# Summing phi(k) over the tokens with a matrix of ones: two fp32 products become four float32r products

## The chip, the cores and the metric

The kernel runs on one core of a Trainium2 chip. The metric is the device time of one execution in microseconds (us), as the median of several runs. The engines are PE (TensorE, the matrix engine), DVE (VectorE), ACT (ScalarE), POOL (GpSimd) and SP (SyncE, which here only issues DMAs); PEld stands for the weight loads of PE. "fp32r" in rows of the profile and "f32r" or "float32r" in the text mean the reduced-precision float32 type of matrix products.

## The reference

Two kinds of block alternate on one sequence of 2048 tokens with 640 channels: A, B, A, B, with the same weights both times, and each block normalizes its input and adds its result to that input.

```python
phi = lambda t: jnp.where(t > 0, t + 1, jnp.exp(t)) + 1e-6
pq, pk = phi(q), phi(k)                       # 32 heads of 20 channels
kv = jnp.einsum("bhsd,bhse->bhde", pk, v)
z = jnp.einsum("bhsd->bhd", pk)               # sum of phi(k) over all tokens
num = jnp.einsum("bhqd,bhde->bhqe", pq, kv)
den = jnp.einsum("bhqd,bhd->bhq", pq, z)[..., None] + 1e-6
o = num / den                                 # then o @ wo
...
r = max(x @ w1 + b1, 0);  out = (r * r) @ w2 + b2     # block B, 1728 hidden
x = x + A(layernorm(x)); x = x + B(layernorm(x))      # twice
```

The change concerns z alone.

## The kernel before

The tokens are 16 tiles of 128 (`NT`), the 640 channels five chunks of 128 (`DC`) or two halves of 320 (`HD`). The kernel goes through two layers; a layer is one block A and one block B. The order of the instructions on each engine is the order of the code: the work is interleaved by hand.

Matrix products are made in float32r from two parts. `split` (L125 to L128) writes a high part, an ACT copy rounded to float32r, and a low part, a DVE subtract of the high part from the source. `mm3` (L379) then makes three products: high by low, low by high, high by high.

Block A goes over the tiles. For each it projects k, and q for most tiles; ACT takes the exponential (L475) and DVE the rest of phi (L482, L483). In `k_post` phi(k) of the tile is split into `kh` (ACT L646, DVE L653), and between the two POOL adds it to the running sum `acc` (L648 for the first tile, L650 for the others): acc[p, c] is the sum over the 16 tiles of phi(k) at row p. With the split normalized input `xh`, PE gathers G and GT, from which k'v is made. The pool function `xtile` hands out eight buffers in rotation to xh and kh, and afterwards to the tiles kvbd, Mr and pT.

For six tiles of each layer q is left out of this loop (`LATE`). These late parts come behind it, two per tile, through `late_q`: 15 products into one of three PSUM banks that `xbank` hands out in rotation, the exponential, the rest of phi, and after the second half a store by SP.

Behind the first two late parts comes the place of the change: a product of a 128x128 matrix of ones with `acc` sums over the 128 rows and puts the sum into every row, so that `zbc` holds z for all partitions.

```python
late_q(2)
zbc = tmp.tile([P, D], F32, tag="z", name="zbc", bufs=1)
psz = [xbank()[:, :HD] for _ in range(2)]
for j in range(2):
    nc.tensor.matmul(psz[j], ones, acc[:, j * HD : (j + 1) * HD], start=True, stop=True)   # L804
for j in range(2):
    nc.scalar.activation(zbc[:, j * HD : (j + 1) * HD], psz[j], AF.Copy)                   # L806
b_den(0)
```

`b_den` (DVE, L582 `pr` and L585 `den`) uses zbc for the denominators. On PE the last G part (`g_part(15)`), the last GT part (added into GT on DVE, L513), another late part, the products for kv (L852) and M (L865) follow, with ACT copies (G of L810, Mc of L871) and small DMAs that shift M into its tiles (Mr); then the first output tiles, whose residual is added on DVE (L621), and ACT's block moves (z of L365), and then block B: fc1 (L1005), fc2 (L1055).

The matrix `ones` is filled by POOL (L539) at the start of each layer. In layer 0 that code stands behind the start-up: the wqkv chunks are loaded (`st`) and split (`kq`, L128), tiles 0 and 1 are normalized (DVE L336, L338, L346 with POOL L340, L341), and tile 1 is transposed on PE (L350) and split into xT.

Of the kernel before, what the change touches and what calls it, by code (L numbers as in the profile page):

```python
# [8 lines left out]
F32 = mybir.dt.float32  # L9
R32 = mybir.dt.float32r  # L10
# [3 lines left out]
P = 128  # L14
# [4 lines left out]
HD = D // 2  # L19
# [52 lines left out]
def kernel(  # L72
# [11 lines left out]
    nc = tc.nc  # L84
# [3 lines left out]
    cpool = ctx.enter_context(tc.tile_pool(name="cpool", bufs=1))  # L88
# [18 lines left out]
    make_identity(nc, ident)  # L107
    neghalf = cpool.tile([P, 1], F32, name="neghalf")
    nc.vector.memset(neghalf, -0.5)
    b2bc = cpool.tile([P, D], F32, name="b2bc")  # L110
    b1sb = cpool.tile([P, NF], F32, name="b1sb")

# [8 lines left out]
    def ftile(name):  # L121
        return tmp.tile([P, D], F32, tag="f", name=name, bufs=F_BUFS)


    def split(hi, lo, src):  # L125

        nc.scalar.activation(hi, src, AF.Copy)
        nc.vector.tensor_tensor(out=lo, in0=src, in1=hi.bitcast(F32), op=ALU.subtract)  # L128
# [283 lines left out]
    def a_load(t, src):  # L412
        if t < NT:
            xt[t] = ftile("xt")
            nc.sync.dma_start(xt[t], src[t])
# [16 lines left out]
    for layer in range(N_LAYERS):  # L432
# [6 lines left out]
        ap = sg.enter_context(  # L439
            tc.tile_pool(name=f"a_{layer}", bufs=1, side="left", reuse_waits="tile")  # L440
        )
# [7 lines left out]
        acc = ap.tile([P, D], F32, name="acc", tag="acc", bufs=1)  # L449
# [4 lines left out]
        def xbank():  # L454
            xbanks.append(xbanks.pop(0))
            return bank(xbanks[-1])

        def part(t, a, b, ps=None):

            ps = (xbank() if ps is None else ps)[:, : b - a]  # L460
            for c in range(DC):
                mm3(
                    ps, xT[t][:, 0, c, :], xT[t][:, 1, c, :],
                    kq[c][:, 0, a:b], kq[c][:, 1, a:b], c == 0, c == DC - 1,
                )
            return ps
# [23 lines left out]
        def xtile(name, dtype=R32):  # L490
            return xp.tile([P, 2, D], dtype, tag="x", name=name, bufs=8)
# [23 lines left out]
        if layer == 0:  # L515
# [19 lines left out]
            a_apply(1)  # L535
            first_loads.step(3, 5)
            a_load(2, src)
        ones = ap.tile([P, P], F32, name="ones", tag="ones", bufs=1)
        nc.gpsimd.memset(ones, 1.0)  # L539
        mask = ap.tile([HR, 6, DH], F32, name="mask", tag="mask", bufs=1)  # L540
        nc.gpsimd.memset(mask, 1.0)

# [235 lines left out]
        def late_q(n=1, rest=True):  # L778

            for _ in range(n):  # L780
                if not late_parts:
                    return
                t, j = late_parts.pop(0)
                if j == 0:
                    late_phi[t] = Phi(ftile("rl"))
                late_phi[t].exp(j * HD, part(t, D + j * HD, D + (j + 1) * HD))
                late_todo.append((t, j))
                if rest:
                    late_rest()
# [3 lines left out]
        def late_rest(n=9):  # L793
            for _ in range(min(n, len(late_todo))):
                t, j = late_todo.pop(0)
                late_phi[t].rest()
                if j == 1:
                    nc.sync.dma_start(pqd[t], late_phi.pop(t).r)

        late_q(2)  # L800
        zbc = tmp.tile([P, D], F32, tag="z", name="zbc", bufs=1)
        psz = [xbank()[:, :HD] for _ in range(2)]
        for j in range(2):
            nc.tensor.matmul(psz[j], ones, acc[:, j * HD : (j + 1) * HD], start=True, stop=True)  # L804
        for j in range(2):
            nc.scalar.activation(zbc[:, j * HD : (j + 1) * HD], psz[j], AF.Copy)  # L806
        b_den(0)
# [729 lines left out]
```

## Time and profile before

| | before |
|---|---|
| time, median of 3 runs | 1353.05 us (1352.7 to 1353.13) |
| time of the profiled execution | 1352.46 us |
| its span, first to last instruction | 1350.5 us |
| granted PE clock | 1.0 |
| PE busy | 1342.5 us |
| DVE busy | 912.1 us |
| ACT busy | 770.2 us |
| POOL busy | 122.6 us |
| the two fp32 products, per layer | 4 records, from 193.10 and from 860.25 us |

Rows of the profile give a start (us from the span's start) and a duration, the engine, the line, the operation and its tiles, out<-in, with partitions x elements; x15 counts instructions. What stands in square brackets is the engine's idle time before it and what ended it. In the chain of work that ended last, each piece is what the end of the kernel was waiting for at that time.

### The profile page before, as it was taken

How to read it: one execution, taken by the hardware profiler on the slowest of the kernel's cores; microseconds unless marked ns; L12 is line 12 of the kernel's file. 1: busy time of each engine (PE TensorE's matmuls, PEld its weight loads, DVE VectorE, ACT ScalarE, POOL GpSimd, SP SyncE). 2: the span in 40 equal slices, each digit the busy share in tenths (PEclk: the TensorE clock that was granted, in tenths of full speed). 3: DMA queues.
4: the chain of work that ended last, by engine and by line, in shares of the span. 5: the costliest groups of instructions: out<-in, count | busy, mean ns of one | idle time of the engine just before them, and what ended most of it. 6: DMA issues, size and time to landing. Idle time of an engine off the chain costs nothing.

```text
span 1350.5 us, 19013 instructions
## 1 busy us (share of the span) xinstructions
PE 1342.5 (99%) x6817; PEld 1160.9 (86%) x6817; DVE 912.1 (68%) x1625; ACT 770.2 (57%) x1931; POOL 122.6 (9%) x174
## 2 busy tenths in 40 slices
PE   9999999999999999999999999999999999999998
PEld 8888998988888888888888899988888888888887
DVE  7888757777777676643467676677778667775323
ACT  5888858566546447411447688495756446464110
POOL 2222210000000000000012232100000000000000
PEclk9999999999999999999999999999999999999999
DMA  6787834574665484387521115156546646654744
GB/s 205 254 296 271 282 92 169 195 280 141 212 242 167 159 297 167 116 326 297 185 98 41 58 40 156 40 205 253 172 160 235 212 148 224 234 168 139 287 126 157
DMA packets 85635, 253.44 MB, mean 188 GB/s; under 512 B 11030, under 2 KB 19606, under 8 KB 84902
## 3 DMA queue, kind: packets, MB, share of 16 engines
q1 hardware_dynamic: 85398, 252.04, 53.8%
q8 instruction: 54, 0.88, 0.3%
q14 instruction: 39, 0.32, 0.1%
q10 hardware_dynamic: 144, 0.20, 0.0%
HBM read 193.50 MB, written 56.03 MB: 185 GB/s over the span
## 4 chain that ended last, share of the span: by engine, by line
PE 92%; DVE 4%; ACT 3%; issue 1%; POOL 0%; DMA 0%; DVEq 0%; ACTq 0%; POOLq 0%
PE PS L379 34%; PE PS L1005 28%; PE PS L1055 28%; ACT z L365 2%; PE PS L852 1%; PE PS L865 1%; DVE bn L336 0%; PE PS L521 0%; DVE kq L128 0%; DVE e L482 0%; DVE xr L621 0%; DVE r L483 0%; DVE xTb L128 0%; DMA Mr<-Mc 0%; POOL rs L341 0%
## 5 line engine op out<-in xcount | busy, mean ns | idle before, releaser
L365 ACT ACTIVATE z<-y 32x160 f32<-32x160 f32 x1424 | 475.9, 334 | 75.7 <-DVE y L356 59.4
L1005 PE MATMUL PS<-xTb,u 128*128 128x512 f32 x1400 | 333.8, 390 | 1.0 <-DVE xTb L128 1.0
L1005 PEld LDWEIGHTS PS<-xTb,u 128*128 128x128 f32 x1400 | 261.7, 188 | 54.9 <-DVE xTb L128 1.5
L379 PE MATMUL PS<-kq,xT 128*128 128x320 f32 (+2 forms) x1635 | 294.0, 334 | 1.1 <-DVE kq L128 0.6
L379 PEld LDWEIGHTS PS<-kq,xT 128*128 128x128 f32 x1635 | 259.0, 188 | 28.9 <-DVE rl L483 1.0
L1055 PE MATMUL PS<-u,h 128*128 128x512 f32 x1120 | 276.8, 390 | 0.0
L1055 PEld LDWEIGHTS PS<-u,h 128*128 128x128 f32 x1120 | 208.6, 188 | 40.8
L1017 ACT ACTIVATE hr<-PS,b1sb 128x512 f32<-128x512 f32 x104 | 71.4, 686 | 295.7 <-PE PS L1005 295.0
L1018 DVE TENSOR_TENSOR hr<-hr 128x512 f32<-128x512 f32 x104 | 71.8, 691 | 218.3 <-ACT hr L1017 217.9
L379 PE MATMUL PS<-kh,xh 128*128 128x512 f32 x480 | 124.3, 393 | 0.0
L475 ACT ACTIVATE e<-PS 128x320 f32<-128x320 f32 (+4 forms) x128 | 53.6, 435 | 102.5 <-PE PS L379 99.0
L340 POOL TENSOR_SCALAR rs<-mv 128x1 f32<-128x1 f32 x64 | 28.0, 438 | 871.1 <-DVE mv L338 871.1
L379 PE MATMUL PS<-uM,pT 128*128 128x320 f32 x648 | 102.6, 309 | 0.7 <-DVE uM L881 0.7
L379 PEld LDWEIGHTS PS<-uM,pT 128*128 128x128 f32 x648 | 97.7, 188 | 3.1 <-DVE uM L881 1.2
L379 PEld LDWEIGHTS PS<-kh,xh 128*128 128x128 f32 x480 | 87.4, 188 | 15.0
L482 DVE TENSOR_SCALAR e<-e 128x320 f32<-128x320 f32 (+4 forms) x128 | 42.6, 333 | 79.6 <-ACT e L475 79.2
L1055 PE MATMUL PS<-h,u 128*128 128x512 f32 x280 | 79.0, 390 | 0.0
L1020 DVE TENSOR_TENSOR h<-hr,h 128x512 fp32r<-128x512 f32 x104 | 72.0, 692 | 3.6
L650 POOL TENSOR_TENSOR acc<-acc,r 128x640 f32<-128x640 f32 x30 | 53.8, 1792 | 199.1 <-DVE r L483 199.1
L1055 PEld LDWEIGHTS PS<-h,u 128*128 128x128 f32 x280 | 52.2, 188 | 10.8 <-DVE h L1031 0.4
L1005 PE MATMUL PS<-xTb,uw 128*128 128x512 f32 x240 | 57.1, 389 | 0.0
L483 DVE SCALAR_TENSOR_TENSOR r<-PS,e 128x512 f32<-128x512 f32 (+2 forms) x104 | 51.1, 492 | 5.8 <-ACT e L475 2.3
(119 smaller groups left out, 1337.6 us busy)
## 6 DMA issues: line engine op xcount, KB each, us to landing
u<-kept_w SPq DMA_DIRECT2D x184, 640.0 KB, 4.7
x<-x SPq DMA_DIRECT2D x48, 320.0 KB, 5.7
kept_w<-uprep SPq DMA_DIRECT2D x23, 640.0 KB, 4.7
pqt<-pq SPq DMA_DIRECT2D x32, 320.0 KB, 4.6
x<-xr SPq DMA_DIRECT2D x32, 320.0 KB, 3.9
st<-in_B_w_dram SPq DMA_DIRECT2D x22, 320.0 KB, 5.8
pq<-r SPq DMA_DIRECT2D x20, 320.0 KB
kept_kq<-kq SPq DMA_DIRECT2D x10, 640.0 KB, 6.8
```

The lines of the kernel that those rows point to most:

```text
L340: nc.gpsimd.tensor_scalar(rs, mv[:, 1:2], LN_EPS, None, op0=ALU.add)
L365: nc.scalar.activation(zv[j * B32 : (j + 1) * B32, :, i, :], yv[i * B32 : (i + 1) * B32, :, j, :], AF.Copy)
L379: nc.tensor.matmul(ps, a, b, start=first and i == 0, stop=last and i == 2)
L475: nc.scalar.activation(self.e[:, a:b], ps, AF.Exp)
L482: nc.vector.tensor_scalar(e, e, 1.0, PHI_EPS, op0=ALU.min, op1=ALU.add)
L483: nc.vector.scalar_tensor_tensor(out=self.r[:, a:b], in0=ps, scalar=0.0, in1=e, op0=ALU.max, op1=ALU.add)
L650: nc.gpsimd.tensor_tensor(out=acc, in0=acc, in1=r, op=ALU.add)
L1005: nc.tensor.matmul(ps, a[:, d, :], bb[:, d, :], start=d == 0 and i == 0, stop=d == DC - 1 and i == len(seq) - 1,)
L1017: nc.scalar.activation(r, ps, AF.Relu, bias=b1sb[:, c : c + 1])
L1018: nc.vector.tensor_tensor(out=r, in0=r, in1=r, op=ALU.mult)
L1020: nc.vector.tensor_tensor(out=h[:, 1], in0=r, in1=h[:, 0].bitcast(F32), op=ALU.subtract)
L1055: nc.tensor.matmul(ps, l, r, start=first and k == 0, stop=last and k == len(a) - 1)
```

## The change

The running sum is split in two parts, as other operands of products are: `ah` holds the float32r copy of acc (ACT) and the rest (DVE). It is made between the first and the second late part. The matrix of ones becomes float32r; it is no longer filled by POOL but copied by DVE from a new constant column of ones. Each half of z is then the sum of two products, ones by the low part and ones by the high part, into one bank.

```diff
@@ constants
     nc.vector.memset(neghalf, -0.5)
+    one = cpool.tile([P, 1], F32, name="one")
+    nc.vector.memset(one, 1.0)
@@ start of each layer
-        ones = ap.tile([P, P], F32, name="ones", tag="ones", bufs=1)
-        nc.gpsimd.memset(ones, 1.0)
+        ones = ap.tile([P, P], R32, name="ones", tag="ones", bufs=1)
+        nc.vector.tensor_copy(ones, one.to_broadcast([P, P]))
@@ behind the loop over the tiles
-        late_q(2)
+        late_q(1)
+        ah = xtile("ah")
+        split(ah[:, 0], ah[:, 1], acc)
+        late_q(1)
         zbc = tmp.tile([P, D], F32, tag="z", name="zbc", bufs=1)
         psz = [xbank()[:, :HD] for _ in range(2)]
         for j in range(2):
-            nc.tensor.matmul(psz[j], ones, acc[:, j * HD : (j + 1) * HD], start=True, stop=True)
+            for i in (1, 0):
+                nc.tensor.matmul(
+                    psz[j], ones, ah[:, i, j * HD : (j + 1) * HD], start=i == 1, stop=i == 0
+                )
```

## The prediction

> **What bounds the kernel now.** I read the page first: busy times, then the chain of work that ended last.
>
> ```profile
> PE 1342.5 (99%) x6817; PEld 1160.9 (86%) x6817; DVE 912.1 (68%) x1625; ACT 770.2 (57%) x1931; POOL 122.6 (9%) x174
> ...
> PE 92%; DVE 4%; ACT 3%; issue 1%; POOL 0%; DMA 0%; DVEq 0%; ACTq 0%; POOLq 0%
> ```
>
> TensorE (PE) holds 92% of that chain and waits almost nowhere, at a granted clock of 1.0 throughout. So time taken off PE where PE carries the chain comes off the end, and a wait put on PE there is added to it. The products that change are those of L804, once per layer. The chain of work in order of time shows them in layer 0:
>
> ```profile
> 180.81 12.46 PE PS L379 x75
> 193.26 1.08 PE PS L804 x4
> 194.34 7.41 PE PS L379 x42
> ```
>
> They lie on the chain, with PE work on both sides. Each fp32 product leaves two records, so 2 products are 4 records and cost 1.08 us. Layer 1 is the same (1.08 us at 860.41). The third view is the timeline around them:
>
> ```profile
> 185.81 0.73 ACT L127 ACTIVATE xh<-xt 128x640 fp32r<-128x640 f32 x1
> ...
> 186.31 0.49 DVE L483 SCALAR_TENSOR_TENSOR r<-PS,e 128x320 f32<-128x320 f32 x1
> 186.72 0.81 DVE L128 TENSOR_TENSOR xh<-xt,xh 128x640 fp32r<-128x640 f32 x1
> ...
> 186.95 2.01 POOL L650 TENSOR_TENSOR acc<-acc,r 128x640 f32<-128x640 f32 x1 [5.67 <-DVE r L483]
> 187.61 2.03 DVE L653 TENSOR_TENSOR kh<-r,kh 128x640 fp32r<-128x640 f32 x1
> ...
> 188.71 4.56 PE L379 MATMUL PS<-kq,xT 128*128 128x320 f32 x30
> 191.10 0.44 ACT L475 ACTIVATE e<-PS 128x320 f32<-128x320 f32 x1 [3.52 <-PE PS L379]
> ...
> 191.93 0.49 DVE L483 SCALAR_TENSOR_TENSOR rl<-PS,e 128x320 f32<-128x320 f32 x1
> 192.96 0.87 PEld L804 LDWEIGHTS PS<-acc,ones 128*128 128x128 f32 x4
> 193.10 1.24 PE L804 MATMUL PS<-acc,ones 128*128 128x320 f32 x4
> ```
>
> The reader sees here all that the change needs: the last addition to acc on POOL is over at 186.95 + 2.01 = 188.96; PE is busy with two late parts (30 products) until L804; an ACT copy and a DVE subtract of the wanted shape stand at 185.81 and 186.72; and the same subtract took 2.03 instead of 0.81 where it ran beside POOL's addition. The last view is the chain at the start of the kernel, since one added instruction lies there:
>
> ```profile
> 15.11 2.47 DVE kq L128 x3
> 17.58 0.25 DVE e L482
> ...
> 19.89 3.44 PE PS L379 x14
> ```
>
> There VectorE (DVE), not PE, carries the chain: PE waits until 19.89 for the low part of xT of tile 1, which stands in DVE's queue behind the three subtracts and the two phi halves.
>
> **The change part by part.**
>
> The products. Thirty f32r products of 320 columns take from 188.71 to 193.10, so 4.39/30 = 0.146 us each. Four are 0.585 us where two fp32 ones took 1.08: **0.50 us less per layer** if nothing waits. The records stay at four per layer. By the Trainium skill (FP8 and Floating Point Precision, TensorE Precision Notes) a true fp32 product is four passes through the array; a pass would then be 1.08/8 = 0.135, four of them 0.54, an estimate, and the saving 0.54 instead of 0.50. The row of the f32r product itself is what I use.
>
> The wait in front of them. Before, L804 waited for POOL's sum, done 4 us earlier. Now its first product needs the low part of ah, that is: exp of the first late part, ACT copy, DVE subtract, PE. ACT's exp starts at 191.10; the copy of xh began 0.33 after the exp ahead of it (185.48 to 185.81), so the copy of ah begins at 191.43 and ends 0.73 later at 192.16. On DVE the subtract stands behind the phi operation of 191.93; at 186.31 the next one began 0.41 later, so it begins at 192.34 (the copy is done by then) and ends 0.81 later at 193.15. From a DVE end to the released weight load of PE the trace shows 0.05 us (h of L1031 ends at 676.72, the load starts at 676.77). So the weight load of L804 starts at 193.20 instead of 192.96: **0.24 us of waiting per layer**. Bounds: nothing, if DVE's part slips under PE's late parts; 1.46 us, if the subtract takes 2.03 as at 187.61. I take 0.24, since POOL has nothing to do here, as at 186.72, where 0.81 was measured.
>
> Who stands behind the waits: on PE, behind L804, the 15 products of the last G part and the ACT evictions of G that they release; they move with it. On ACT the copy lies in an idle stretch of 1.76 us ahead of the second exp (193.30), which it leaves at 192.16. On DVE the subtract lies in an idle stretch of 1.35 us ahead of 193.77 and is over at 193.15, so the store of the late phi on SP and the first pr are not later. The copies of zbc (193.84, 194.3) need the first two products, ready at about 193.34 + 0.29 + 0.2 = 193.8 as before. All of that costs nothing; if the cover on ACT or DVE were gone, each step would cost its own 0.73 or 0.81 on PE.
>
> Net at this place: -0.50 + 0.24 = -0.26 per layer, **-0.51** for two. What follows is a chain of PE work (G, kv, M) released by PE itself until 219, and the DVE and ACT work after it is released by PE, so the shift should reach the end.
>
> The matrix of ones. POOL loses a fill of 0.20 us per layer; POOL is idle 91% of the span, so nothing is gained. DVE gets a copy of 128x128 with rounding. In layer 1 it stands behind the residual additions that end at 681.1, and DVE is idle until 683.89: nothing. In layer 0 it stands between the third kq subtract (ends 17.58) and the phi operation of 17.50, on the chain. The trace has no such copy. A DVE operation of 128x128 took 0.23 (L482 at 686.97), a fill of one column 0.06; neighbours overlap by 0.08 there. Between 0.06 and 0.23 I take 0.23 - 0.08 = **+0.15 us**, nearest to the row of equal size. The new one-column fill at the start runs while DVE waits until 3.93 for x: nothing.
>
> The tile ah takes the place of an old xh tile, and the later tiles of that pool (kvbd, Mr, pT) each move on by one place. Their former owners are read last by the G and GT parts that end near 200, and the new users come after 202: nothing. The new column of ones moves nearly all other SBUF tiles by 32 bytes (tmp tiles from offset 224 to 0 within 256). I cost that at nothing; it is a rival below.
>
> Sum: -0.51 + 0.15 = **-0.36 us**. The profiled execution took 1352.46 (span 1350.5 and 1.96 around it), so it would be 1352.1; it lies 0.59 under the median of 1353.05, and for the median I forecast 1353.05 - 0.36 = **1352.7**. A difference of 0.2%, 2.7 us, is about what a measurement of this kernel can tell from no change, and the sum is far inside it.
>
> **The rivals.**
>
> 1. No wait: the subtract ends before PE asks for it. Then 2 x 0.50 is gained and 0.15 paid, -0.84: **1352.2**. For it: only 0.24 us are missing. Against: the chain exp, copy, subtract is laid end to end from measured rows.
>
> 2. The gain does not arrive: the wait is 0.50, or the stretch from 237 to 242, where ACT's z moves carry the chain, takes back what PE gained. Left is the +0.15 of the start: **1353.2**. Against: that stretch is released by PE's product through the addition of L621.
>
> 3. Slower by a late subtract: if it runs at the 2.03 of 187.61, PE waits 1.46 instead of 0.24, +0.96 per layer, with the start +2.1: **1355.1**. It costs more than the products save from a duration of 0.81 + 0.26 = 1.07 on. For it: 2.03 is there, 5 us earlier, for an equal subtract. Against: that one lay beside POOL's addition, and the last addition is over 3.4 us before this one. The Trainium skill (SBUF — State Buffer, Who interferes with whom) has a rule for it: a DVE instruction with two SBUF inputs contends with a GpSimd instruction that reads SBUF. The trace agrees with it in the pair 186.95/187.61; it would decide only if POOL's addition ended 3.4 us later.
>
> 4. The moved addresses change the rate of every product. Column time from two rows: 15 products of 512 columns take 3.40 us (0.227 each) against 0.146 for 320, so 0.081/192 = 0.42 ns a column. One column time over 6817 records is 2.9 us. One less gives -3.2: **1349.8**; two more give +5.3: **1358.4**. For it: all f32r operands of this trace start at the same offset, so no row shows another. Against: on DVE and ACT, r (offset 192) and xt (224) cost the same, 0.81 and 0.73 to 0.75. The skill's DMA: Bandwidth & Descriptors (How a descriptor splits into AXI transactions) counts an extra transaction where a descriptor does not start on 256 B; that would shorten transfers now, but no run here shows it so far, and DMA holds 0% of the chain.
>
> That the change does not do what it says I exclude: every f32r product of 320 columns in the trace takes the 0.146.
>
> **How the numbers follow.** The forecast has 0.56; rival 1 0.15, a quarter microsecond away; rival 2 0.10; rival 3 0.04, as its cause is absent; rival 4 0.09 for faster and 0.06 for slower, since the trace can't exclude it and either sign is open. Forecast and rivals 1 and 2 span 1352.2 to 1353.2 and hold 0.81; with the scatter of the runs (1352.46 to 1353.13) and the unknown wait (0.24 us more per layer than I took is +0.5) the range is 1351.2 to 1354.2. Rivals 3 and 4 stay outside. Faster by over 0.2%: 0.09 (rival 4). Slower: 0.06 (rival 4). Within: 0.56 + 0.15 + 0.10 + 0.04 = 0.85.
>
> **What would show it.** In the profile after: four records on ah and ones, spaced 0.146 and not 0.27; their weight load 0.24 us later than before, counted from the first late part, with a wait on DVE's ah; that subtract at 0.81 (rival 3: 2 us); the chain's piece at these products down from 1.08 to some 0.6 plus 0.24 of DVE; PE's first product after xT of tile 1 about 0.15 later than 19.89; POOL 172 instructions, DVE 1630, ACT 1933. If 15 products of 512 columns no longer take 3.40, it is rival 4. The prediction is wrong if the time moves by more than 2 us either way.

## The result and the profile after

| | before | after |
|---|---|---|
| time, median of 6 runs each | 1352.93 us (1352.7 to 1353.22) | 1364.74 us (1364.3 to 1364.94) |
| ratio, after to before | | 1.0086 (95%: 1.0076 to 1.0096) |
| profiled execution, its span | 1352.46, 1350.5 us | 1364.3, 1362.5 us |
| granted PE clock | 1.0 | 0.999 |

The changed kernel is 11.8 us slower, and the forecast of 1352.7 us with its range of 1351.2 to 1354.2 was wrong. What the change itself does came out almost as worked out; the time went to products that the change does not touch.

The page of the kernel after, its busy times, the shares of the chain, and three rows of the costliest groups (row columns: busy us, mean ns of one | idle time ahead of it):

```profile
PE 1354.2 (99%) x6817; PEld 1160.0 (85%) x6817; DVE 913.8 (67%) x1630; ACT 771.2 (57%) x1933; POOL 122.4 (9%) x172
...
PE 91%; DVE 3%; ACT 3%; DMA 1%; issue 1%; POOL 0%; SPq 0%; DVEq 0%; ACTq 0%
...
L1013 PE MATMUL PS<-xTb,u 128*128 128x512 f32 x1400 | 334.9, 391 | 1.0 <-DVE xTb L130 1.0
...
L1063 PE MATMUL PS<-u,h 128*128 128x512 f32 x1120 | 282.6, 394 | 0.0
...
L1063 PE MATMUL PS<-h,u 128*128 128x512 f32 x280 | 80.7, 397 | 0.0
```

PE has the same 6817 records and 11.7 us more busy time (1342.5 to 1354.2); the other engines moved by under 2 us. So the time is not a new wait: it is inside PE's own work. The same rows of the page before:

```profile
L1005 PE MATMUL PS<-xTb,u 128*128 128x512 f32 x1400 | 333.8, 390 | 1.0 <-DVE xTb L128 1.0
...
L1055 PE MATMUL PS<-u,h 128*128 128x512 f32 x1120 | 276.8, 390 | 0.0
...
L1055 PE MATMUL PS<-h,u 128*128 128x512 f32 x280 | 79.0, 390 | 0.0
```

fc2 (u,h and h,u) alone has 5.8 + 1.7 = 7.5 us more, with as many products as before. The place that the change was made for looks as forecast. The chain after, in order of time, in layer 0:

```profile
181.84 12.48 PE PS L381 x75
194.32 0.80 PE PS L810 x4
195.12 7.37 PE PS L381 x42
```

The four records cost 0.80 instead of 1.08 us, and the 75 products ahead of them 12.48 instead of 12.46. The timeline after around them:

```profile
192.16 0.44 ACT L477 ACTIVATE e<-PS 128x320 f32<-128x320 f32 x1 [3.55 <-PE PS L381]
192.49 0.73 ACT L129 ACTIVATE ah<-acc 128x640 fp32r<-128x640 f32 x1
...
192.99 0.49 DVE L485 SCALAR_TENSOR_TENSOR rl<-PS,e 128x320 f32<-128x320 f32 x1
193.39 0.81 DVE L130 TENSOR_TENSOR ah<-acc,ah 128x640 fp32r<-128x640 f32 x1
194.26 0.59 PEld L810 LDWEIGHTS PS<-ah,ones 128*128 128x128 f32 x4 [0.21 <-DVE ah L130]
194.26 0.85 PE L810 MATMUL PS<-ah,ones 128*128 128x320 f32 x4
```

exp, copy, subtract and weight load follow each other as laid out: copy 0.33 after the exp, subtract at 0.81 and not 2.03, a wait of 0.21 on DVE's ah. And the chain after at the start of the kernel:

```profile
15.18 2.48 DVE kq L130 x3
17.65 0.14 DVE ones L541
17.79 0.24 DVE e L484
...
20.10 3.48 PE PS L381 x14
```

The copy of ones costs 0.14 us on DVE's chain; PE's first product of tile 1 starts at 20.10 instead of 19.89. All of this together is a fraction of a microsecond. The chain in the middle of block B of layer 0 shows the rest, 15 products a piece, first before:

```profile
333.90 3.40 PE PS L1005 x15
337.30 3.40 PE PS L1055 x15
```

and then after:

```profile
335.59 3.41 PE PS L1013 x15
339.00 3.50 PE PS L1063 x15
```

fc1 (L1013) runs as before, fc2 (L1063) takes 0.10 us more for every 15 products. Summed over the trace, from the start of one PE product to the start of the next (u are the streamed weights of block B and uw those that stay in SBUF, kq,xT the projections of block A, uM,pT its output product):

| group, moving operand first | spacings | before | after | difference |
|---|---|---|---|---|
| fc2 u,h 512 columns | 1119 | 227.5 ns | 232.6 ns | +5.80 us |
| fc2 h,u 512 | 280 | 228.3 | 234.1 | +1.62 |
| fc2 uw,h and h,uw 512 | 240 | 226.7 | 232.8 | +1.48 |
| fc1 xTb,u and xTb,uw 512 | 1640 | 227.5 | 228.4 | +1.34 |
| kq,xT 512 | 570 | 228.0 | 230.3 | +1.31 |
| kq,xT 320 | 780 | 151.6 | 152.0 | +0.29 |
| uM,pT 320 | 648 | 148.4 | 148.6 | +0.15 |

Together these are 12.0 us, as much as the span grew (the groups left out, the start and the gain at the changed place are each under 0.6 and nearly cancel); 11.6 of it is in products of 512 columns. A 512-column product takes 226.7 ns in its fast form (uw,h before), and near 233 in its slow one.

### The profile page after: what moved, and what is told of

Same layout as the page of the kernel before. It is cut to its first block, busy times and chain, and to the rows that moved or that the text cites. A ratio compares the mean times of both kernels' runs of the same rounds, so it can differ in the third digit from the quotient of the medians.

```text
span 1362.5 us, 19015 instructions
## 1 busy us (share of the span) xinstructions
PE 1354.2 (99%) x6817; PEld 1160.0 (85%) x6817; DVE 913.8 (67%) x1630; ACT 771.2 (57%) x1933; POOL 122.4 (9%) x172
## 4 chain that ended last, share of the span: by engine, by line
PE 91%; DVE 3%; ACT 3%; DMA 1%; issue 1%; POOL 0%; SPq 0%; DVEq 0%; ACTq 0%
PE PS L381 33%; PE PS L1063 28%; PE PS L1013 27%; ACT z L367 2%; PE PS L860 1%; DMA st<-in_A_wqkv_dram 1%; PE PS L873 1%; DVE bn L338 0%; DVE e L484 0%; DVE xr L623 0%; DVE r L485 0%; DVE xTb L130 0%; DMA Mr<-Mc 0%; PE PS L1077 0%; POOL rs L343 0%
## 5 line engine op out<-in xcount | busy, mean ns | idle before, releaser
L1013 PE MATMUL PS<-xTb,u 128*128 128x512 f32 x1400 | 334.9, 391 | 1.0 <-DVE xTb L130 1.0
L1013 PEld LDWEIGHTS PS<-xTb,u 128*128 128x128 f32 x1400 | 261.7, 188 | 56.3 <-DVE xTb L130 1.5
L1063 PE MATMUL PS<-u,h 128*128 128x512 f32 x1120 | 282.6, 394 | 0.0
L1063 PEld LDWEIGHTS PS<-u,h 128*128 128x128 f32 x1120 | 208.3, 187 | 47.0
L1063 PE MATMUL PS<-h,u 128*128 128x512 f32 x280 | 80.7, 397 | 0.0
L1063 PEld LDWEIGHTS PS<-h,u 128*128 128x128 f32 x280 | 52.2, 188 | 11.6 <-DVE h L1039 0.3
L1013 PE MATMUL PS<-xTb,uw 128*128 128x512 f32 x240 | 57.2, 390 | 0.0
```

The costliest lines, as they stand in the source:

```text
L1013: nc.tensor.matmul(ps, a[:, d, :], bb[:, d, :], start=d == 0 and i == 0, stop=d == DC - 1 and i == len(seq) - 1,)
L1063: nc.tensor.matmul(ps, l, r, start=first and k == 0, stop=last and k == len(a) - 1)
```

## The experiments

SBUF tiles are handed out from both ends of a partition, left-hand pools upwards and right-hand ones downwards. Theory A: the new column of ones shifts the other tiles of the left-hand side of SBUF by 32 bytes, against the tiles of block B's pool, which lie on the right-hand side (weights u on the left, h on the right), and that makes 512-column products slower. The rival, theory P: the work that the change adds or moves (split, copy of ones, the four products) does it.

**The column of ones alone** (to the kernel before):

```diff
+    one = cpool.tile([P, 1], F32, name="one")
+    nc.vector.memset(one, 1.0)
```

> The kernel before with nothing but the new constant column of ones and its fill: the products, the split and the matrix of ones stay as before, but nearly all tiles of the left-hand pools start 32 bytes later, as in the changed kernel. Theory A (addresses: the moved tiles slow the float32r products, the products of ones are nearly free): about 1365, fc2 products spaced 232 to 234 ns instead of 227. Theory P (the new products, split or copy disturb PE's rhythm, addresses don't matter): 1352.9, spacing 227.

Measured: 1365.37 us against 1352.99, ratio 1.0092 (1.0075 to 1.0108). One unused column costs all of it.

**The whole change, with addresses as before** (to the kernel after: the ones share a tile with a constant that was there):

```diff
-    neghalf = cpool.tile([P, 1], F32, name="neghalf")
+    consts = cpool.tile([P, 2], F32, name="consts")
+    neghalf = consts[:, 0:1]
...
-    one = cpool.tile([P, 1], F32, name="one")
+    one = consts[:, 1:2]
```

> The changed kernel with both one-column constants in one tile of two columns, so that every other tile keeps the address it had before. Theory A: the local sum of the prediction comes out, about 1352.6 (0.36 less than before), fc2 spacing 227. Theory P: 1364.7, spacing 232 to 234.

Measured: 1352.81 against 1352.99, 0.9998 (0.9988 to 1.0007). The loss is gone, and the change by its work alone is not to be told from no change. Its chain in layer 0:

```profile
181.38 12.45 PE PS L382 x75
193.84 0.80 PE PS L811 x4
194.64 7.38 PE PS L382 x42
```

From the start of the 75 products to the end of the four records it is 13.26 us; before it was 13.53 (180.81 to 194.34). So 0.27 us per layer are gained, where 0.26 were forecast. Theory P is ruled out: by the interval, what the change adds or moves costs at most 1 us of the 11.8. What in the addresses does it was open.

**One column more, and the right-hand side moved as well.** Before, both sides begin 224 bytes into a stretch of 256; after, the left one 0. One more padding tile on the left gives 32 and 224:

```diff
+    pad = cpool.tile([P, 1], F32, name="pad")
+    nc.vector.memset(pad, 1.0)
```

> The changed kernel with one more column tile, so that the left-hand tiles lie 64 bytes behind their old places instead of 32 (offset 32 within 256). Theory A with a period of 64 bytes: 1352.6, as if nothing had moved. Theory A with a longer period or with 224 as the one good offset: slow, around 1364. Theory P: 1364.7.

A padding tile on the right (which grows downwards) gives 0 and 192:

```diff
+    rpool = ctx.enter_context(tc.tile_pool(name="rpool", bufs=1, side="right"))
+    rpad = rpool.tile([P, 1], F32, name="rpad")
+    nc.vector.memset(rpad, 1.0)
```

> The changed kernel with the right-hand pools (xh, kh, ah, h, pT, x1) moved by 32 bytes too, by a column tile at that end: left-hand tiles at offset 0, right-hand at 192 within 256. Theory A as a matter of the two operands' relative offset within 64: 1352.6, spacing 227. Theory A as a matter of the left-hand tiles' own offset (0 is bad): 1364.7. Theory P: 1364.7.

Measured: 1360.31 (1.0054, 1.0039 to 1.0069) and 1360.07 (1.0052, 1.0037 to 1.0067). Neither number was expected: a tile's own offset does not decide, nor does a distance within 64 bytes. But the two agree, and what they share is the distance between the sides, 192 bytes one way and 64 the other. From here on theory R: what counts is the distance of a product's two operands, the address of the stationary one less that of the moving one, modulo 256 bytes.

**Block B's pool alone** (to the kernel after; a padding tile of one column ahead of block B's tiles on the right, so only these lie 32 bytes lower):

```diff
+        rp = sb.enter_context(
+            tc.tile_pool(name=f"bpad_{layer}", bufs=1, side="right", reuse_waits="tile")
+        )
+        bpad = rp.tile([P, 1], F32, name="bpad")
+        nc.vector.memset(bpad, 1.0)
```

> The changed kernel with only the right-hand pool of block B (h, x1, pT) moved by 32 bytes: distance 64 in block B, 32 in block A. Theory R with the spacings measured at distance 64: fc2's 1311 products with u moving fall from 232.6 to about 229.6, 3.9 us less, fc1 gets 0.3 more: about 1361. If block A carried the loss: 1364.7, no change.

Measured: 1360.78, 1.0056 (1.0041 to 1.0071): as the two before it, so the distance from the left-hand tiles to block B's counts.

**The right-hand padding alone, in the kernel before** (the three lines of `rpad`, nothing of the change):

> The kernel before, with no part of the change: only a column tile at the other end, which moves the right-hand pools by 32 bytes against the left-hand ones, the same distance as in the changed kernel. Theory R: 1365.4, like the kernel with only the new column of ones. Rival (the left-hand tiles' own offset counts): 1353.0.

Measured: 1365.03, 1.009 (1.0075 to 1.0105). Its timeline of PE in block B:

```profile
335.73 3.58 PE L1008 MATMUL PS<-xTb,u 128*128 128x512 f32 x15
339.15 2.95 PE L1058 MATMUL PS<-u,h 128*128 128x512 f32 x12
341.94 0.86 PE L1058 MATMUL PS<-h,u 128*128 128x512 f32 x3
```

From start to start, the 12 u,h take 2.79 us. Nothing of the left-hand side moved here, and nothing of the change is in it.

**Both sides at offset 0, 256 bytes of distance instead of 0** (to the kernel after, a right-hand padding of 224 bytes):

```diff
+    rpool = ctx.enter_context(tc.tile_pool(name="rpool", bufs=1, side="right"))
+    rpad = rpool.tile([P, 56], F32, name="rpad")
+    nc.vector.memset(rpad, 1.0)
```

> The changed kernel with the right-hand pools moved by 224 bytes, so that both sides lie at offset 0 within 256 (distance 256 instead of 32). Theory R (what counts is the distance of a product's two operands, moving and stationary, within 256 bytes): 1352.8, as with the addresses of before; fc2 spacing 227. Rival (224 is the good offset, or the distance counts beyond 256): above 1357.

Measured: 1352.48 against 1353.29, 0.9995 (0.9985 to 1.0004). The shift of the left-hand side is all there, and the time is back:

```profile
334.20 3.56 PE L1016 MATMUL PS<-xTb,u 128*128 128x512 f32 x15
337.60 2.88 PE L1066 MATMUL PS<-u,h 128*128 128x512 f32 x12
340.32 0.84 PE L1066 MATMUL PS<-h,u 128*128 128x512 f32 x3
```

The 12 u,h take 2.72 us again. A distance of 256 bytes is as good as none.

**The distance by itself.** A kernel without the layers: groups of 24 products of 512 columns, one moving operand, a stationary one read at a distance o from it, modulo 256 bytes (`k % 2` switches between two places 1024 bytes apart).

```python
for n, o in enumerate(OFFS):
...
    for k in range(N_EACH):
        d = o // 4 + 256 * (k % 2)
        nc.tensor.matmul(ps, sta[:, d : d + P], mov[:, :512], start=k == 0, stop=k == N_EACH - 1)
```

> No part of the layers: 57 groups of 24 float32r products of 512 columns, moving operand fixed, stationary operand at a distance of 0 to 248 bytes in steps of 8 and 256 to 1024 in steps of 32 from it (within 1024). Output is the input, so the time itself means nothing. Theory R: spacing 227 ns at distance 0, 256, 512, 768 and 1024, about 234 at 32 and 64, 229.6 at 192 and 232.6 at 224 (as fc2 shows with the roles either way), the same again in each 256. If the distance of the two operands does not matter: 227 in all groups.

Mean spacing of the last 12 products of a group:

| distance, bytes | 0 | 8 | 24 | 32 to 72 | 96 | 120 | 128 | 176 | 192 | 224 | 240 |
|---|---|---|---|---|---|---|---|---|---|---|---|
| ns | 227.0 | 230.5 | 230.0 | 233.3 | 234.3 | 226.7 | 233.3 | 230.0 | 228.9 | 233.3 | 226.7 |

and 226.7 again at 256, 512, 768 and 1024. Beyond 256, in steps of 32, the values repeat within 0.3 ns, except that 384, 640 and 896 gave 231.7 where 128 gave 233.3. Two of its groups in the timeline, at 256 and 288 bytes (the transposes stand between groups):

```profile
207.49 5.74 PE L85 MATMUL PS<-mov,sta 128*128 128x512 f32 x24
213.06 0.49 PE L81 MATMUL PS<-ident 128*128 128x128 f32 x3
213.31 5.84 PE L85 MATMUL PS<-mov,sta 128*128 128x512 f32 x24
```

The same operation, with the same operands but for their distance, is 0.10 us per 24 longer. The table also fits the kernels. With stationary less moving operand, the column of ones gives 224 for u,h and 32 for h,u: 233.3 by the table, 232.6 and 234.1 in the kernel after. The two kernels of the third experiment give 192 and 64: 228.9 and 233.3 by the table, 229.6 and 233.8 in the one with two columns.

**Half the stretch** (to the kernel after, `rpad` of 24 columns, a distance of 128):

> The changed kernel with the right-hand pools moved by 96 bytes: the two sides 128 bytes apart within 256. Theory R with the table of distances (233.3 ns at distance 128, either way round): fc2's products all at 233.3, so a little slower than at 32, where u before h gives 232.6: about 1365. If half the period were as good as the whole: 1352.8.

Measured: 1366.89 against 1353.03, 1.0103 (1.0084 to 1.0121), the slowest of all. fc2's u,h are at 232.9 ns, its h,u at 231.5 where the table has 233.3, and fc1's xTb,u, both from the left-hand side, at 230.4 (227.7 before). In the middle of block B the first nine of fc1's 15 products scatter between 224 and 236 ns and only then settle at 227; in the kernel after, only the first one (232.5) and the last one are off. So what a group does to the next one has a part as well, and the table alone does not give the time of a kernel.

The borders between runs of products show more. In the kernel after, where fc1 ends and fc2 begins, and where the 12 u,h end:

```profile
338.61 0.40 PE L1013 MATMUL PS<-xTb,u 128*128 128x512 f32 x1
338.61 0.19 PEld L1063 LDWEIGHTS PS<-u,h 128*128 128x128 f32 x1
338.84 0.39 PE L1063 MATMUL PS<-u,h 128*128 128x512 f32 x1
...
341.41 0.19 PEld L1063 LDWEIGHTS PS<-h,u 128*128 128x128 f32 x1
```

The weights of a product (PEld) are loaded while the product before it runs: h for the first u,h beside the last fc1 product, u for the first h,u beside the last u,h. That last fc1 product takes 235 ns, although its own operands are both on the left (mean of 99 runs 234.5, before 226.9). The last of 12 u,h takes 226.6 (mean of 87 runs), although its own operands are on different sides; the other eleven take 230.8 to 235.0. So these rows point to the moving operand of one product and the stationary operand of the next. The load records themselves take 188 ns in both kernels. At a distance of 128 the last u,h stays slow (233.1), so this reading does not cover everything.

**Widths** (the kernel without layers again, six distances at five widths):

> No part of the layers: float32r products with moving operands of 512, 448, 384, 320 and 256 columns, each with the stationary operand at distances of 0, 32, 64, 128, 192 and 224 bytes. Output is the input. Theory R as so far seen in the kernels: at 512 columns 226.7 at 0 and up to 233.3 elsewhere; at 320 and 256 hardly any difference (the products of 320 kept their mean of 148.5 in all kernels). If the extra belongs to every weight load, whatever the product beside it: 6.6 ns more at every width.

| columns | spacing at 0, 32, 64, 128, 192, 224 bytes, ns |
|---|---|
| 512 | 229.9 (16 records found), 233.3, 233.3, 232.9, 228.9, 233.3 |
| 448 | 206.7, 203.3, 202.2, 204.2, 200.0, 206.7 |
| 384 | 173.3, but 175.6 at 128 |
| 320 | 146.7 to 146.8 |
| 256 | 120.0, 118.2, 113.3, 118.8, 117.8, 116.7 |

Two groups of 320 and two of 448 columns in its timeline, at 0 and 32 bytes and at 0 and 192:

```profile
53.63 5.20 PE L85 MATMUL PS<-mov,sta 128*128 128x448 f32 x24
...
74.54 5.06 PE L85 MATMUL PS<-mov,sta 128*128 128x448 f32 x24
...
112.01 3.76 PE L85 MATMUL PS<-mov,sta 128*128 128x320 f32 x24
...
115.85 3.77 PE L85 MATMUL PS<-mov,sta 128*128 128x320 f32 x24
```

Products of 320 columns do not care, in keeping with the 320-column groups of block A, which lost next to nothing; so the extra does not belong to every weight load. The spread at 256 columns was not expected, and at 448 and 256 columns distance 0 is not the best one.

**The best version that came out of it**: addresses as before, and the copy of ones on POOL, off DVE's chain.

```diff
-        nc.vector.tensor_copy(ones, one.to_broadcast([P, P]))
+        nc.gpsimd.tensor_copy(ones, one.to_broadcast([P, P]))
```

> The changed kernel with all addresses as before (both constants in one tile) and the matrix of ones copied by POOL instead of DVE: DVE's copy of 0.14 leaves the chain at the start. By the sum of the prediction without its +0.15: 0.51 to 0.6 less than before, about 1352.4. If the start is set by the loads anyway: as with DVE's copy, 1352.8.

Measured: 1352.72 against 1353.03, 0.9998 (0.9989 to 1.0007). At the start the chain no longer holds the copy:

```profile
15.71 2.47 DVE kq L131 x3
18.18 0.25 DVE e L485
```

but the whole start lies 0.6 us later than in the kernel before (15.11), with the landing of the weights (its chain there holds their DMA from 7.69 to 14.28), so the 0.14 us that the copy cost can't be seen in the time. No version is measurably faster than the kernel before.

## Why the prediction was wrong

- **Products**, -0.50 us per layer: the chain's piece of 0.80 us is four times 0.146 and the wait of 0.21 below. Right. (That "every" product of 320 columns takes 0.146 was read too narrowly, the groups lie between 0.146 and 0.149 without their waits, but nothing hangs on it.)
- **The wait**, +0.24 per layer: 0.21, ended by DVE's ah, with every step at the duration taken for it. Right, and so was the net of -0.26 per layer (-0.27 with the addresses as before).
- **Copy of ones**, +0.15: 0.14 on the chain, taken as 0.23 less an overlap of 0.08. Right.
- **Counts**: PE 6817, DVE 1630, ACT 1933, POOL 172, as forecast.
- **Rivals 1 to 3**: there was a wait, the subtract ran at 0.81, and the gain arrived at this place (with the addresses as before). Whether it reached the end is not shown: the interval of that run, 0.9988 to 1.0007, holds the forecast and rivals 1 and 2 alike.
- **"The new column of ones moves nearly all other SBUF tiles by 32 bytes (tmp tiles from offset 224 to 0 within 256). I cost that at nothing"**: this is the step that failed, a term put at nothing. With the column alone the kernel is 12.4 us slower, and with the whole change but no shift it is not measurably slower.

Rival 4 named the cause, moved addresses, but sized it wrongly, gave it 0.06 on the slow side and stood outside the range. Its price was one or two column times (0.42 ns) on each of the 6817 records, 1358.4 us at most. In truth it is up to 233.3 - 226.7 = 6.6 ns, 16 column times, on products of 512 columns whose two operands come from different sides: 1639 products of fc2 at 5 to 7 ns each are 8.9 us. Another 2.65 us lie on fc1 and on the 512-column kq,xT, whose two operands moved together; of fc1's 1.34 us nearly all is in the first and the last product of its runs (5.7 and 7.6 ns more, 99 runs). The 320-column groups of the table lost 0.44 us. The sign that the prediction gave for this rival came true: 15 products of fc2 take 3.50 us and no longer 3.40. "All f32r operands of this trace start at the same offset, so no row shows another" was the sentence to stop at. Taken seriously it says that these operand pairs all stood at distance 0 modulo 256, and the trace could bound no other. The row set against it (r and xt cost the same on DVE and ACT) was of other engines; the products of PE had no row.

By the Trainium skill (TensorE: Matmul & The Clock Gate, Step-by-step: what each phase is for) the loading of the next weights takes no SBUF bandwidth from the running product, since each has a read port, and by the Trainium skill (SBUF — State Buffer, Who interferes with whom) "PE and ACT never wait on anyone". By these rules the shift costs nothing. The measurement decides otherwise: the same product took 226.7 or 233.3 ns with nothing changed but the distance of its two operands.

What stays open is how it comes about. That the read of the moving operand and the next weight load meet in the same part of SBUF fits three things: a period of 256 bytes, the dependence on the distance alone, and the fast and slow products at the borders of runs. But no experiment separated the weight load from the product, so this is argued and not shown. Nor is it shown why 120 and 240 bytes are fast, or why the first products after a change of operands run slow for a while even at distance 0.

## What to carry to other kernels

A new small tile is not free because nobody waits for it: a column of 4 bytes took 32 bytes of each partition and moved everything allocated after it, which cost some thirty times the gain that was forecast (11.8 against 0.36 us). Put such a constant into a tile that is there, as the second experiment did, and where a kernel's products come from two sides of SBUF, look at the distance of their operands modulo 256 bytes before and after a change; distance 0 was a good one at 512 columns, not at every width. When a trace shows only one value of something that the change alters, it bounds nothing, and the range has to say so.

## What the hardware showed that was not expected

- A steady stream of float32r products of 512 columns runs at 226.7 to 227.0 ns with its two operands 0, 120, 240, 256, 512, 768 or 1024 bytes apart, and mostly at 230 to 234 ns at other distances, with a period of 256 bytes in what was tried (but for 128, 233.3 once and 231.7 three times).
- Products of 320 columns took 146.7 ns at each distance tried; at 448 columns 200.0 (192 bytes) to 206.7 (0 and 224), at 256 columns 113.3 (64 bytes) to 120.0 (0): the good distance depends on the width.
- After a change of operands a run of such products can take up to ten products to settle (224 to 236 ns in the kernel with a distance of 128), so a group's cost also depends on what stands ahead of it.
- At the border of two runs, a product's time went with the stationary operand that is loaded for its successor: 234.5 ns for the last fc1 product with h to be loaded, 226.6 for the last u,h with u to be loaded.
